# One more product in two levels, and three stages interleaved, in a linear-attention and tanh-shrink kernel

## Chip, cores, metric

The kernel runs on one core of one Trainium2 chip. The metric is the device time of one execution in microseconds; lower is better. Everything is f32.

## What is computed

The reference is a blockwise linear attention with decay, whose output, reordered to tokens by features, goes through a feed-forward block with the activation h - tanh(h):

```python
for b in range(nb):                                     # blocks of the sequence
    qb, kb, vb = (q[:, :, sl], k[:, :, sl], v[:, :, sl])
    intra = np.einsum('bhic,bhjc->bhij', qb, kb) * Dmask[None]
    intra = np.einsum('bhij,bhjd->bhid', intra, vb)
    inter = np.einsum('bhid,bhde->bhie', qb * lam_pow[None], kv_state)
    out[:, :, sl] = intra + inter
    kv_state = lam_block[None, :, None, None] * kv_state + np.einsum('bhsd,bhse->bhde', kb_dec, vb)
x = np.ascontiguousarray(attn_out.transpose(0, 2, 1, 3)).reshape(B * S, H * D)
h = x @ w_in
g = h - np.tanh(h)
return (g @ w_out).astype(np.float32)
```

Shapes: q, k and v are (4, 8, 768, 64), so x has 3072 tokens of 512 features; w_in is 512 x 2048 and w_out is 2048 x 512.

## The kernel before

The tokens are worked in six groups of 512 (128 positions of each of the 4 batches). While group g goes through the feed-forward block, attention for group g + 1 is run in pieces between its products: transposes and scores of two batches, then output and state, then the same for the other two (L381).

From group 1 on both matrix products use the Strassen-Winograd scheme: each operand is cut in 2 x 2 quarters, and seven products P1 to P7 of sums of quarters (`FACT`, L386) take the place of eight. Both the first product (tokens by w_in, `up`, L406) and the second (`down`, L602, and `down_twice`, L649) go that way. The first works per unit: there are NU = 4 units of 512 columns of w_in, and a product of one unit is 4 matmuls of 128 x 128 weights over 256 tokens. P1, P6 and P7 accumulate on one PSUM bank ("ya" or "yb"), P5 and P3 on "z"; what stands in a bank after each step is read by ScalarE or VectorE into the hidden tiles `hidden(g, c)`, with c = 11, 12, 21, 22 for the quarters of the result. The tanh and the subtraction are in `finish` (L421). Product P3 (L450) completes quarter 12, after which VectorE forms the sums S1 and S2 that the second product needs (L454, L455).

Some of the seven products are themselves computed by the same scheme a second time ("in two levels"): a product then consists of seven steps of 4 matmuls of 128 x 128 weights over 128 columns, in the order `STEPS = (1, 2, 6, 5, 7, 3, 4)`. In the second product these are P4 to P7 and P3 (`TWICE`), except some in the first and last groups; in the first product, from group GI = 2 on, they are P2 and P4 (`INNER`). `inner(g)` computes P2 and P4 together, a step of one and a step of the other in turn, before unit 0 starts. Weights for these steps that are sums of quarters are prepared once, in group 1, by `inner_weights` (L465) and written to DRAM (`fine_in`); the sums of tokens are formed per group by `inner_tokens` (L475).

Weights for the second product, and the sums for the steps 6, 5 and 3 of the two-level parts of the first, are streamed from DRAM as pieces of 256 KB in a ring of RING = 7 buffers. The order in which they are wanted is written out beforehand in `pieces_of` (L525); `piece` (L565) issues loads on POOL's queue up to seven pieces ahead. A buffer is loaded again when the matmuls that read it are done. Results are stored from POOL's queue too (L590). In the second product's P4 to P7 and P3, step x = 3 needs quarter a12 minus a sum, formed in place by VectorE at L666 after step 2 has read a12.

The order of the work in a group is the main loop's:

```python
for u in range(NU):
    for n in (2, 6, 5, 7, 1, 4, 3) if g < GI else (6, 5, 1, 7, 3) if u + 1 < NU else (6, 5, 7, 1, 3):
        ...            # n == 1: P1 of the next unit, and after the last unit the second product's P1
# then the second product: P2, P4, P5, P6, P7 with attention pieces between them, and
inner_tokens(g + 1)
down_twice(g, 3, "z")
inner(g + 1)
up(g + 1, 0, 1)
```

The instructions of each engine run in the order of its queue, which the tile framework makes from this program; operations marked `keep_in_program_order` stay where they are.

Of the kernel before, what the change touches and what calls it, by code (L numbers as in the profile page):

```python
# [23 lines left out]
def kernel(  # L24
# [32 lines left out]
    nc = tc.nc  # L57
# [129 lines left out]
    fine_in = dram.tile([2, 3, 128, NU, 128], F32, name="fine_in")  # L187
# [203 lines left out]
    def product_bank(key, n):  # L391

        if n == 1:
            banks[key, "y"] = bank("y", "yb" if key[0] == "up" and key[2] % 2 else "ya", 1)
        if n in (2, 5):
            banks[key, "zw"[n == 2]] = bank("zw"[n == 2], "zw"[n == 2], 1)
        t = banks[key, {2: "w", 5: "z", 3: "z"}.get(n, "y")]
        return t.rearrange("q (m c) -> q m c", m=2), n in (1, 2, 5)
# [7 lines left out]
    def up(g, u, n):  # L406
# [23 lines left out]
        elif g >= GI and n == 5:  # L430
            nc.scalar.activation(dst(22), z, AF.Copy)
        elif g >= GI and n == 7:
            nc.vector.tensor_tensor(dst(22), dst(22), y, op=AL.add)
            nc.vector.tensor_tensor(dst(21), dst(21), y, op=AL.add)
            finish(22, dst(22))
            finish(21, dst(21))
        elif n == 1:
            nc.scalar.activation(dst(11), y, AF.Copy)
        elif n == 2:
            nc.vector.tensor_tensor(dst(11), dst(11), w, op=AL.add)  # L440
            finish(11, dst(11))
        elif n == 6:
            nc.scalar.activation(dst(12), y, AF.Copy)
        elif n == 7:
            nc.scalar.activation(dst(22), y, AF.Copy)
            nc.vector.tensor_tensor(dst(22), dst(22), z, op=AL.add)
            finish(22, dst(22))
        elif n == 4:
            finish(21, y)
        elif n == 3:  # L450
            nc.vector.tensor_tensor(dst(12), dst(12), z, op=AL.add)
            finish(12, dst(12))

            nc.vector.tensor_tensor(dst("S1"), dst(12), dst(22), op=AL.add)  # L454
            nc.vector.tensor_tensor(dst(12), dst(11), dst(12), op=AL.subtract)  # L455
# [6 lines left out]
    def a_quarter(n, u, i, k):  # L462
        return w1[u][:, 2 + k, INNER.index(n), ts(i, 128)]

    def inner_weights(u):  # L465
        for n in INNER:
            a11, a12, a21, a22 = (a_quarter(n, u, i, k) for i in range(2) for k in range(2))
            t = late["pool"].tile([128, 4, 128], F32, name="ws2", tag="sums", bufs=4)
# [4 lines left out]
            nc.gpsimd.dma_start(out=fine_in[INNER.index(n)].rearrange("x p u c -> p u x c")[:, u], in_=t[:, 0:3])  # L473

    def inner_tokens(g):  # L475
        for n in INNER:
# [10 lines left out]
    def inner(g):  # L487

        y, w, z, r5 = {}, {}, {}, {}
        for n, tag in zip(INNER, ("yb", "ya")):  # L490
            y[n] = bank("y3", tag, 1)
            w[n], z[n] = (bank(x, "att", 4) for x in ("w3", "z3"))
            r5[n] = otile("r5")
        for x in STEPS:
            for n in INNER:
                out4 = hidden(g, 11 if n == 2 else 21)
                c11, c12, c21, c22 = (out4[:, :, i, ts(j, 128)] for i in range(2) for j in range(2))
                b = toks[g, n][x]
                wb = piece(g, ("in", n), x) if x in (3, 5, 6) else None
                dst = w[n] if x == 2 else z[n] if x in (3, 5) else y[n]  # L500
                for u in range(NU):
                    a = wb.rearrange("p m c -> p (m c)")[:, ts(u, 128)] if wb is not None else a_quarter(
                        n, u, *{1: (0, 0), 2: (0, 1), 7: (1, 0), 4: (1, 1)}[x])
                    nc.tensor.matmul(out=dst[:, ts(u, 128)], lhsT=a, rhs=b, start=x in (1, 2, 5) and u == 0, stop=True,  # L504
                                     skip_group_check=True)
                d = dst.rearrange("q (u c) -> q u c", u=NU)
                if x in (1, 4, 6):
                    nc.scalar.activation({1: c11, 4: c21, 6: c12}[x], d, AF.Copy)  # L508
                elif x == 5:
                    nc.scalar.activation(r5[n], dst, AF.Copy)  # L510
                elif x == 7:
                    nc.vector.tensor_tensor(c22, r5[n].rearrange("q (u c) -> q u c", u=NU), d, op=AL.add)
                else:
                    c = c11 if x == 2 else c12
                    nc.vector.tensor_tensor(c, c, d, op=AL.add)
# [8 lines left out]

    def pieces_of(g):  # L525
        if g >= GI:
            yield from ((g, ("in", n), x) for x in (6, 5, 3) for n in INNER)
        if g == 2:
            yield from ((g, ("quarter", t), x) for t in (3, 4) for x in range(4))
        for n in (1, 2, 4, 5, 6, 7, 3):  # L530
            yield from ((g, n, x) for x in (SUB if twice(g, n) else range(NU)))

# [32 lines left out]
    def piece(g, n, x):  # L565

        i = stream.index((g, n, x))
        while sent["n"] < min(i + RING, len(stream)):
# [5 lines left out]
            elif isinstance(n_, tuple):  # L574
                nc.gpsimd.dma_start(out=t.rearrange("p m c -> p (m c)"), in_=fine_in[
                    INNER.index(n_[1]), (5, 6, 3).index(x_)].rearrange("p u c -> p (u c)"))
# [24 lines left out]

    def down(g, n):  # L602

        if n in (1, 2):
            t, first = product_bank(("down", g), n)
        else:
            t, first = bank("plain", "w" if n == 7 else "z", 1).rearrange("q (m c) -> q m c", m=2), True
        a = hidden(g, HIDAT[FACT[n][0]])
        for u in range(NU):
            wb = piece(g, n, u)  # L610
            for m in range(2):
                for kt in range(2):
                    nc.tensor.matmul(out=t[:, m, :], lhsT=a[:, u, kt, ts(m, 128)], rhs=wb[:, kt, :],  # L613
                                     start=first and u == 0 and m == 0 and kt == 0, stop=u == NU - 1 and kt == 1,
                                     skip_group_check=True)
        t = t.rearrange("q m c -> q (m c)")
# [32 lines left out]
    def down_twice(g, n, zw):  # L649
# [6 lines left out]
        for x, a, dst, keep in ((1, a11, y, o[:, 0:128]), (2, a12, zw[:, 0:128], None), (6, s2, y, o[:, 128:256]),  # L656
# [8 lines left out]
            if x == 2:  # L665
                nc.vector.tensor_tensor(a12, a12, s2, op=AL.subtract)  # L666
        nc.vector.tensor_tensor(o[:, 384:512], o[:, 384:512], r5, op=AL.add)
# [11 lines left out]
        elif n == 3:  # L679
            nc.vector.tensor_tensor(o, o, res[g, 5], op=AL.add)  # L680
            store(g, 12, o)

# [83 lines left out]
    turns, made = {1: (0, (7, 14, 21)), 2: (7 * NU, (2, 7))}, []  # L766
# [3 lines left out]
    for g in range(1, NG):  # L770
        last = g == NG - 1
        p0, p1 = attention(g + 1) if not last else ([], [])
        for u in range(NU):
            for n in (2, 6, 5, 7, 1, 4, 3) if g < GI else (6, 5, 1, 7, 3) if u + 1 < NU else (6, 5, 7, 1, 3):
                if n != 1:
                    up(g, u, n)
                elif u + 1 < NU:
                    up(g, u + 1, 1)
                else:
                    down(g, 1)  # L780
# [10 lines left out]
            if g == GI - 1:  # L791
                inner_weights(u)
# [3 lines left out]
        down(g, 2)  # L796
        run(p0[2:])
        sums_twice(g, 5)
        down_twice(g, 4, "z")
# [3 lines left out]
        down_twice(g, 5, "w")  # L803
# [3 lines left out]
        down_twice(g, 6, "z")  # L807
# [3 lines left out]
        if twice(g, 7):  # L811
            down_twice(g, 7, "w")
        else:
            down(g, 7)
        if not last:
            if g + 1 >= GI:
                inner_tokens(g + 1)
            else:
                up(g + 1, 0, 1)
            if twice(g, 3):  # L820
                down_twice(g, 3, "z")
            else:
                down(g, 3)
            if g + 1 >= GI:
                inner(g + 1)
                up(g + 1, 0, 1)
        else:
            down_end(g)
# [30 lines left out]
```

## Time and profile before

| | us |
|---|---|
| median of 3 runs | 678.91 (676.9 to 679.36) |
| the profiled execution | 680.09 |
| its span | 678.3 |
| group 1 (155.2 to 265.4) | 110.2 |
| group 2 (265.4 to 371.5) | 106.1 |
| group 3 (371.5 to 477.8) | 106.3 |
| group 4 (477.8 to 582.0) | 104.2 |
| group 5 (582.0 to 678.0) | 96.0 |

Each group is counted from its first matmul of the first product (for group 1, of the first unit). The granted TensorE clock was 1.00 in all five. DMA moved 129.59 MB; 256 KB pieces took a median of 4.1 us (two-level weights of the second product), 4.4 (one-level) and 5.4 (fine_in) from issue to landing.

How to read the lines quoted later. A group line names source line, engine, operation, what is written and read, the shape and the count. A line of the timeline has start and length in us, then the engine, line and operation; in brackets stands the idle time of the engine before it and what ended it. A line of the windows has the stretch and its length, then the busy time of TensorE, of its weight loads (PEld), VectorE (DVE), ScalarE (ACT) and GpSimd (POOL), the granted clock, the busy share of the DMA engines and GB/s.

### The profile page before, as it was taken

To read this page: it belongs to the slowest core of one execution; us is meant where nothing else is said; L and a number is where in the kernel's file an instruction comes from. 1 tells how busy PE (TensorE), PEld (TensorE's weight loads), DVE (VectorE), ACT (ScalarE), POOL (GpSimd) and SP (SyncE) were. 2 spreads that over 40 slices of the span, in tenths; PEclk is the share of its full clock that TensorE was granted. 3 is DMA by queue.
4 is the path that set the end of the run, shared out by engine and by line. 5 is a ranking of instruction groups with operands and counts; after the bars stand their busy time and mean duration, and the time that the engine had idled before them with its cause. 6 is when DMAs were issued, how large, how long until landed. Compare 5 with 4: busy or idle time off the path is not lost.

```text
span 678.3 us, 12940 instructions
## 1 busy us (share of the span) xinstructions
PE 662.7 (98%) x4832; PEld 575.2 (85%) x4832; DVE 482.0 (71%) x878; ACT 201.3 (30%) x398; POOL 201.5 (30%) x348
## 2 busy tenths in 40 slices
PE   6899999999999999999999999999999999999997
PEld 5788855558888899988999988899988899988897
DVE  3797858894889962588986378887358977357753
ACT  2664432423331211343112343112333122334120
POOL 0001424216444434421345200255300244500261
PEclk9999999999999999999999999999999999999999
DMA  9869979958957978686698641698821676700494
GB/s 187 227 195 236 287 215 257 301 142 248 263 173 215 259 208 202 160 238 136 180 277 266 192 82 43 153 284 244 246 42 36 153 240 206 249 22 1 112 303 159
DMA packets 162957, 129.59 MB, mean 191 GB/s; under 512 B 133904, under 2 KB 135056, under 8 KB 162896
## 3 DMA queue, kind: packets, MB, share of 16 engines
q0 software_dynamic: 29216, 97.28, 45.6%
q1 hardware_dynamic: 133536, 31.50, 23.4%
q8 instruction: 38, 0.62, 0.4%
q14 instruction: 23, 0.19, 0.1%
q10 hardware_dynamic: 144, 0.00, 0.0%
HBM read 104.34 MB, written 24.38 MB: 190 GB/s over the span
## 4 chain that ended last, share of the span: by engine, by line
PE 69%; issue 15%; POOL 6%; DMA 6%; DVE 3%; ACT 1%; SPq 0%; POOLq 0%; DVEq 0%; ACTq 0%
PE y L415 13%; PE op L719 8%; PE z L415 8%; PE y L661 7%; PE h L703 6%; PE zw L661 5%; POOL wb L578 5%; PE y L504 3%; PE w L613 3%; PE y L613 3%; PE sp L313 3%; DMA wb<-fine 2%; PE plain L613 2%; DMA raw<-in_moe_w_in_dram 2%; PE op L364 2%
## 5 line engine op out<-in xcount | busy, mean ns | idle before, releaser
L578 POOL DMA_DIRECT2D wb<-fine x154 | 82.9, 538 | 122.0 <-PE y L661 46.3
L423 ACT ACTIVATE th<-g 128x512 f32<-128x512 f32 x76 | 47.3, 630 | 104.5 <-DVE g L428 35.6
L581 POOL DMA_DIRECT2D wb<-factors x52 | 28.2, 543 | 162.0 <-PE y L613 118.1
L415 PE MATMUL y<-xt,w 128*128 128x256 f32 x320 | 73.5, 380 | 0.0
L415 PEld LDWEIGHTS y<-xt,w 128*128 128x128 f32 x320 | 60.5, 190 | 9.4 <-ACT g L508 0.9
L424 DVE TENSOR_TENSOR g<-g,th 128x512 f32<-128x512 f32 x76 | 52.0, 689 | 22.5 <-ACT th L423 22.2
L664 ACT ACTIVATE q<-y 128x128 f32<-128x128 f32 x88 | 24.4, 277 | 115.8 <-PE y L661 114.0
L703 PE MATMUL h<-xt,w 128*128 128x256 f32 x256 | 56.2, 381 | 1.1 <-DVE w L270 1.1
L719 PE MATMUL op<-wt,g 128*128 128x512 f32 x128 | 56.5, 596 | 0.0
L703 PEld LDWEIGHTS h<-xt,w 128*128 128x128 f32 x256 | 48.3, 190 | 8.5 <-DVE w L270 1.5
L661 PE MATMUL y<-wb,g 128*128 128x128 f32 x408 | 54.4, 278 | 1.0 <-DMA wb<-fine 1.0
L661 PEld LDWEIGHTS y<-wb,g 128*128 128x128 f32 x408 | 49.3, 192 | 2.4 <-issue 1.5
L719 PEld LDWEIGHTS op<-wt,g 128*128 128x128 f32 x128 | 23.8, 190 | 27.7 <-issue 26.5
L415 PE MATMUL z<-tt,ws 128*128 128x256 f32 x160 | 38.7, 380 | 0.0
L317 DVE TENSOR_TENSOR ss<-sp,mask 128x512 f32<-128x512 f32 x48 | 30.8, 681 | 10.6 <-PE sp L313 10.6
L415 PE MATMUL y<-tt,ws 128*128 128x256 f32 x160 | 38.2, 382 | 0.0
L415 PE MATMUL z<-xt,ws 128*128 128x256 f32 x160 | 37.9, 380 | 0.0
L661 PE MATMUL zw<-wb,g 128*128 128x128 f32 x272 | 36.1, 276 | 0.6 <-DMA wb<-fine 0.5
L197 POOL DMA_DIRECT2D raw<-in_moe_w_out_dram x16 | 8.8, 553 | 92.7 <-ACT r L261 59.9
L613 PE MATMUL w<-wb,g 128*128 128x256 f32 x160 | 35.8, 382 | 0.0
L613 PE MATMUL y<-wb,g 128*128 128x256 f32 x160 | 35.4, 379 | 0.0
L415 PEld LDWEIGHTS y<-tt,ws 128*128 128x128 f32 x160 | 30.1, 190 | 5.4 <-DVE g L428 1.5
(169 smaller groups left out, 1290.5 us busy)
## 6 DMA issues: line engine op xcount, KB each, us to landing
wb<-fine POOLq DMA_DIRECT2D x154, 256.0 KB, 4.1
wb<-factors POOLq DMA_DIRECT2D x60, 256.0 KB, 4.4
raw<-in_moe_w_out_dram POOLq DMA_DIRECT2D x16, 512.0 KB, 5.1
v_nat<-in_v_dram SPq DMA_DIRECT2D x24, 256.0 KB, 5.3
factors<-wt POOLq DMA_DIRECT2D x8, 768.0 KB, 5.5
wb<-fine_in POOLq DMA_DIRECT2D x24, 256.0 KB, 5.4
k_nat<-in_k_dram SPq DMA_DIRECT2D x20, 256.0 KB, 5.4
raw<-in_moe_w_in_dram SPq DMA_DIRECT2D x8, 512.0 KB, 5.8
```

Source lines behind the costliest of these rows:

```text
L313: nc.tensor.matmul(out=sp[j][:, p, :], lhsT=kt[ts(j, 64), p, :], rhs=qt[ts(j, 64), p, :], start=True, stop=True)
L317: nc.vector.tensor_tensor(ss[:, j], sp[j], mask[:, j], op=AL.mult)
L415: nc.tensor.matmul(out=t[:, m, :], lhsT=wt[:, kt, ts(m, 128)], rhs=x[:, kt, :], start=first and m == 0 and kt == 0, stop=kt == 1, skip_gro ...
L423: nc.scalar.activation(th, src, AF.Tanh)
L424: nc.vector.tensor_tensor(dst(c), src, th, op=AL.subtract)
L578: nc.gpsimd.dma_start(out=t.rearrange("p m c -> p (m c)"), in_=fine[TWICE.index(n_), SUB.index(x_)].rearrange("p u c -> p (u c)"))
L581: nc.gpsimd.dma_start(out=t, in_=factors[XAT[FACT[n_][1]]][:, 2 * x_:2 * x_ + 2, :])
L613: nc.tensor.matmul(out=t[:, m, :], lhsT=a[:, u, kt, ts(m, 128)], rhs=wb[:, kt, :], start=first and u == 0 and m == 0 and kt == 0, stop=u = ...
L661: nc.tensor.matmul(out=dst, lhsT=a[:, u, :], rhs=wb[:, ts(u, 128)], start=x in (1, 2) and u == 0, stop=u == NU - 1, skip_group_check=True)
L664: nc.scalar.activation(keep, dst, AF.Copy)
L703: nc.tensor.matmul(out=hm[:, m, :], lhsT=w1[u][:, i, a, ts(m, 128)], rhs=xt[0, t][:, i, :], start=m == 0 and i == 0, stop=i == KI - 1, ski ...
L719: nc.tensor.matmul(out=obank[b], lhsT=g, rhs=wt[:, 2 * a:2 * a + 2, :], start=kt == 0 and a == 0, stop=kt == KH - 1 and a == 1)
```

## The change

P3 of the first product is computed in two levels from group 2 on. It leaves the unit loop; its seven steps are run once for all four units, in turn with the four units of the second product's P1 (`inner_last`). P2 of the next group is run in turn with P3 of the second product, step by step (`in_turn`), and P4 of the next group in turn with P1, P6 and P5 of its unit 0 and P1 of its unit 1. The weight stream is reordered to match. The sums of weights for P3 are written by `inner_weights` in group 1, its sums of tokens are formed at unit 1. The addition of P5 to quarter 12, part of P3's work before, moves to P5 in the unit loop. The banks of the unit's products change ("w", "ya", "yb", "w" for units 0 to 3), and the last two sets of second-product weights made in group 2 get their turns at other places. `down` and `down_twice` become generators, so that a caller can take one step at a time.

```diff
     def product_bank(key, n):
         if n == 1:
-            banks[key, "y"] = bank("y", "yb" if key[0] == "up" and key[2] % 2 else "ya", 1)
+            tag = "ya" if key[0] == "down" else ("w", "ya", "yb", "w")[key[2]] if key[1] >= GI else ("ya", "yb")[key[2] % 2]
+            banks[key, "y"] = bank("y", tag, 1)
...
         elif g >= GI and n == 5:
             nc.scalar.activation(dst(22), z, AF.Copy)
+            nc.vector.tensor_tensor(dst(12), dst(12), z, op=AL.add)
...
-    def inner(g):
+    def inner_step(g, n, x, dst):
+        b = toks[g, n][x]
+        wb = piece(g, ("in", n), x) if x in (3, 5, 6) else None
+        for u in range(NU):
+            a = wb.rearrange("p m c -> p (m c)")[:, ts(u, 128)] if wb is not None else a_quarter(
+                n, u, *{1: (0, 0), 2: (0, 1), 7: (1, 0), 4: (1, 1)}[x])
+            nc.tensor.matmul(out=dst[:, ts(u, 128)], lhsT=a, rhs=b, start=x in (1, 2, 5) and u == 0, stop=True,
+                             skip_group_check=True)
+        return dst.rearrange("q (u c) -> q u c", u=NU)
+
+    def inner_steps(g, n, tag):
+        y, w, z, r5 = bank("y3", tag, 1), bank("w3", "att", 4), bank("z3", "att", 4), otile("r5")
...
+    def inner_last(g):
+        y, w, z = (bank("y3", "yb", 1), bank("w3", "w", 1), bank("z3", "z", 1))
+        def quarter_of(c, i, j):
+            return hidden(g, c)[:, :, i, ts(j, 128)]
+        for step in (0, (1, 0, 0), (2, 0, 0), 1, (6, 0, 1), (5, 1, 1), 2, (7, 1, 1), (3, 0, 1), 3, (4, 1, 0)):
+            if isinstance(step, int):
+                down_unit(g, 1, step)
+                continue
+            x, i, j = step
+            c = quarter_of(12, i, j)
+            d = inner_step(g, 3, x, w if x == 2 else z if x in (3, 5) else y)
+            nc.vector.tensor_tensor(c, c, d, op=AL.add)
+            if x in (2, 7, 3, 4):
+                th = work.tile([128, NU, 128], F32, name="th2", tag="th")
+                nc.scalar.activation(th, c, AF.Tanh)
+                nc.vector.tensor_tensor(c, c, th, op=AL.subtract)
+                nc.vector.tensor_tensor(quarter_of("S1", i, j), c, quarter_of(22, i, j), op=AL.add)
+                nc.vector.tensor_tensor(c, quarter_of(11, i, j), c, op=AL.subtract)
+        down_end_of(g, 1)
...
+    def in_turn(g):
+        if twice(g, 3):
+            return [a for x in STEPS for a in (("down", x), ("in", x))]
+        return [("down", 0), ("in", 1), ("in", 2), ("down", 1), ("in", 6), ("in", 5), ("down", 2), ("in", 7), ("in", 3),
+                ("down", 3), ("in", 4)]
...
     def pieces_of(g):
         if g >= GI:
-            yield from ((g, ("in", n), x) for x in (6, 5, 3) for n in INNER)
+            yield from ((g, ("in", 4), x) for x in (6, 5, 3))
...
-        for n in (1, 2, 4, 5, 6, 7, 3):
+        for n in (1, 2, 4, 5, 6, 7):
+            if g >= GI and n == 1:
+                yield from ((g, 1, 0), (g, 1, 1), (g, ("in", 3), 6), (g, ("in", 3), 5), (g, 1, 2), (g, ("in", 3), 3),
+                            (g, 1, 3))
+                continue
             yield from ((g, n, x) for x in (SUB if twice(g, n) else range(NU)))
...
+        for kind, x in in_turn(g):
+            if kind == "down":
+                yield g, 3, x
+            elif x in (3, 5, 6):
+                yield g + 1, ("in", 2), x
...
-    turns, made = {1: (0, (7, 14, 21)), 2: (7 * NU, (2, 7))}, []
+    turns, made = {1: (0, (7, 14, 21)), 2: (7 * NU, (1, 5))}, []
...
-            for n in (2, 6, 5, 7, 1, 4, 3) if g < GI else (6, 5, 1, 7, 3) if u + 1 < NU else (6, 5, 7, 1, 3):
+            if g >= GI and u == 1:
+                inner_tokens(g, (3,))
+            for n in (2, 6, 5, 7, 1, 4, 3) if g < GI else (7,) if u == 0 else (6, 1, 5, 7) if u + 1 < NU else (
+                    6, 5, 7, 1):
                 if n != 1:
                     up(g, u, n)
+                elif g >= GI and u + 1 == NU:
+                    inner_last(g)
...
             if g == GI - 1:
-                inner_weights(u)
+                inner_weights(u, INNER)
+                for uu in ((), (), (0, 1), (2,))[u]:
+                    inner_weights(uu, (3,), False)
...
-            if twice(g, 3):
-                down_twice(g, 3, "z")
-            else:
-                down(g, 3)
-            if g + 1 >= GI:
-                inner(g + 1)
-                up(g + 1, 0, 1)
+        inner_tokens(g + 1, INNER)
+        p3 = down_twice(g, 3, "z") if twice(g, 3) else down(g, 3)
+        p2 = inner_steps(g + 1, 2, "yb")
+        for kind, _ in in_turn(g):
+            next(p3 if kind == "down" else p2)
+        every(p2)
+        every(p3)
+        p4 = inner_steps(g + 1, 4, "yb")
+        for n in (None, None, 1, None, None, 6, None, None, -1, None, 5):
+            if n is None:
+                next(p4)
+            else:
+                up(g + 1, n < 0, abs(n))
+        every(p4)
```

`inner_steps` reads the banks as `inner` did; the sums of weights of the last unit for P3 are made after the second product's P4 in group 1. New code places L666 of `down_twice` at L722.

## The prediction

> **What bounds the kernel now.** I read the busy table first, then the windows of one group, then TensorE's timeline inside it, and VectorE's and the DMAs' only where TensorE loses time.
>
> ```profile
> PE 662.7 (98%) x4832; PEld 575.2 (85%) x4832; DVE 482.0 (71%) x878; ACT 201.3 (30%) x398; POOL 201.5 (30%) x348
> ```
> ```profile
> 265.40:371.50 106.10, 105.93 (x874) 97.36 (x873) 81.57 (x139) 28.44 (x61) 39.51 (x69) 1.00 0.76 207
> ```
>
> The second line is group 2, from its first two-level matmul to that of group 3: TensorE 105.93 of 106.10 us, VectorE 81.57. But VectorE's mean hides a stretch from 306 to 334 us in which it pauses for well under 2 us. Two prices come from TensorE's timeline:
>
> ```profile
> 311.30 7.07 PE L613 MATMUL y<-wb,g 128*128 128x256 f32 x32
> 318.21 1.89 PE L415 MATMUL z<-xt,ws 128*128 128x256 f32 x8
> 371.45 1.06 PE L504 MATMUL y<-xt,w 128*128 128x128 f32 x8
> 372.34 1.06 PE L504 MATMUL y<-tt,w 128*128 128x128 f32 x8
> ```
>
> An f32 matmul leaves two records. From start to start, 32 records of 256 columns take 318.21 - 311.30 = 6.91 us, so a unit's product (4 matmuls) costs 1.73; 8 records of 128 columns take 0.89, the price of a two-level step (4 matmuls). Time above these prices is what TensorE lost. Three places matter:
>
> ```profile
> 277.86 1.03 PE L415 MATMUL z<-tt,ws 128*128 128x256 f32 x4
> 278.72 1.98 PE L415 MATMUL y<-xt,w 128*128 128x256 f32 x8
> 280.54 1.03 PE L415 MATMUL z<-tt,ws 128*128 128x256 f32 x4
> 281.54 1.99 PE L415 MATMUL y<-tt,ws 128*128 128x256 f32 x8
> 283.37 3.62 PE L415 MATMUL y<-xt,w 128*128 128x256 f32 x16
> ...
> 476.80 1.13 PE L661 MATMUL y<-wb,g 128*128 128x128 f32 x8 [0.98 <-DMA wb<-fine]
> ```
> ```profile
> 234.75 0.71 DVE L293 STREAM_TRANSPOSE kt<-k_blk 128x512 f32<-128x512 f32 x1 [1.41 <-DMA k_nat<-in_k_dram]
> 235.39 0.65 DVE L303 TENSOR_TENSOR qd<-qt,fwd 128x512 f32<-128x512 f32 x1
> 235.96 0.68 DVE L666 TENSOR_TENSOR gS<-gS,s 128x512 f32<-128x512 f32 x1
> ...
> 335.07 0.69 DVE L666 TENSOR_TENSOR g<-g,s 128x512 f32<-128x512 f32 x1 [0.59 <-PE zw L661]
> ```
>
> Unit 0: P5, P1, P6 need 24 records x 0.216 = 5.18 us and take 283.37 - 277.86 = 5.51. Weights: the last step of the second product's P3 in group 3 waits for its load. VectorE: in group 1 TensorE's next step x=3 starts at 236.74, just after the L666 at 235.96 that it needs, so there VectorE already sets the pace. In group 2 the same instruction waits for TensorE.
>
> **What the Trainium skill says.** "Perfetto Trace Analysis", Identifying the Most-Contended Engine, holds matmul busy time a poor measure and points to LDWEIGHTS; here that row is 85%, and the even start-to-start times show TensorE full all the same. "TensorE: Matmul & The Clock Gate", Back-to-back issue gap, has the spacing of short matmuls set by the weight load as well, so that half the columns cost more than half; the trace agrees in kind (0.216 against 0.111 a record). "VectorE: DVE Perf Modes", The perf-mode tier table, keeps f32 tensor_tensor at its base rate from SBUF and PSUM alike; the trace agrees (689 ns on L424 from SBUF, 0.69 on L451 from PSUM, some 0.60 between starts in a full queue). "DMA: Bandwidth & Descriptors", Anatomy of one DMA, gives 2.0 us plus bytes over 436 GB/s, an estimate of 2.6 us for 256 KB; the trace has 4.1 for the two-level weights and decides.
>
> **The change part by part.**
>
> 1. *P3 in two levels, groups 2 to 5.* Removed: 4 units x 1.73 = 6.91 us a group. Added: 7 steps x 0.89 = 6.25. TensorE is the path, so 4 x -0.66 = **-2.6 us**.
>
> 2. *P4 in turn with unit 0, and no P3 in the unit loop.* P6 of unit 0 then has two P4 steps (1.79 us) between itself and P1, whose L428 must first read the bank; the 0.33 us above goes, and it is the same in groups 3, 4 and 5: 1.3, I take -1.2. P5 also waits for its bank z before unit 2 in groups 2 and 4 (0.30 and 0.23 over price), because P3 sat in that bank; now P5's result leaves by one copy and one addition, three products ahead: -0.5. Together **-1.7** (0 to -1.8).
>
> 3. *P3 of the second product in turn with P2.* Now 7 weight pieces in 6.25 us, then 6 in the 12.5 us of P2 and P4 together. After: 10 pieces in the first 12.5 us, 3 in P4. A ring of 7 gives a load 7 steps, 6.25 us; waiting on POOL and issue take about 0.9 of them, and landing 4.1 (5.9 in the bad case). Spread out it has about 8.7. So the 1.15 us of group 3 and 0.37 of group 2 mostly go: **-1.2** (0 to -1.6). The stores of q4 and q7 stay where they were in POOL's queue behind the weights; P2's r5 copy needs q4's slot, whose store is issued at 366.70 and lands 4.8 later, about 371.5; that copy comes 7.1 us after P7's end at 364.8, so 371.9, and TensorE needs it only 2.7 us after that. Free, with cover.
>
> 4. *VectorE's queue in groups 2 to 4.* Per group 16 operations leave the units (four of L451 to L455 in each); in come 4 additions of z in the units, 7 of steps, and 3 for each of 4 quarters: 23. Worse than 7 x 0.60 is where they go: 19 of them stand in P3's 13.2 us with P1 (7 x 0.89 + 4 x 1.73), besides unit 3's leftovers. Walking the compiled order of group 3 from the end of unit 3's P7 (time 0) at 0.60 an operation: the transposes begin at -2.4 instead of -0.8; P7's two reads end at 3.05, and step x=2, which reuses their bank, can start at 3.5: 0.4 to spare. The scores' products end at 19.8 (wanted at 23.4), both k_nat at 24.0 (wanted 25.3), L666 of P4 at 30.7 (wanted 30.9), and that of P5, behind six operations of the transposes, at 37.8 (wanted 37.2). So 0.6 us of stall in groups 2 and 3; in group 4 there is no state to update (four operations, 2.4 us, fewer; there L666 waits 2.26 us for TensorE now), so none. **+1.2** (0 if operations overlap better; +4 if the queue is a microsecond later).
>
> 5. *Group 1: three times the inner weights.* 16 more small operations (281 ns long, 0.20 between starts), 12 of them before the scores, 2.4 us in a VectorE queue that hardly pauses from 195 to 230; 1.3 us of pauses near 210 absorb about half. The two L666 at 227.60 and 235.96 both already hold TensorE, so what remains lands on it. The 4 extra writes of fine_in (0.75 us each on POOL) stand ahead of weight pieces, each waiting for its VectorE operations. **+1.5** (0 to +3). The 12 more loads and 4 writes, about 3.9 MB of 129.6, fall mostly where the DMA row reads 42 to 82 GB/s: nothing. The later turn of the last two factors costs nothing, their VectorE work only changes unit.
>
> 6. *New waits.* Steps of P3 alternate with P1's units, so a bank gets 2.6 us between two writes, against 0.7 for a read. ScalarE is 30% busy. In P4 the bank of P2 is taken over after one step (0.89) against a copy of 0.60 plus its start. I take **+0.5** for a few tenths lost somewhere (0 to +2).
>
> Sum: -2.6 - 1.7 - 1.2 + 1.2 + 1.5 + 0.5 = -2.3. The profiled execution took 680.09 us (span 678.3 and 1.8 around it), so 677.8; the median shown is 678.91, 1.2 less, which puts the forecast at **676.6**.
>
> **The rivals.**
>
> *All of it hides.* VectorE's pauses take up parts 4 to 6. For: VectorE at 71% over the span. Against: the stretch from 306 to 334 us. 678.91 - 5.5 + 0.2 = 673.6.
>
> *The waits of unit 0 and of the weights only move.* Then parts 2 and 3 bring nothing: -2.6 + 3.2 = +0.6, 679.5. For: the DMA row is at 244 to 284 GB/s in the stages of the two-level second product, which stay. Against: the steps that waited are now apart.
>
> *VectorE becomes the bound after P3 (slower).* The place is L666 of P4 and P5 in groups 2, 3 and 4. My walk leaves it no reserve, so every further microsecond of lag is one of TensorE's. An operation that depends on the one before it starts 0.72 us after it (L454 to L455: 300.54 to 301.27), not 0.60, and a quarter's chain crosses ScalarE, 1.44 us from addition to subtraction. If half the 19 pay for it, about 2.5 us a group: three groups +7.5, and 678.91 - 2.3 + 7.5 = 684.1. It decides from 1.9 us a group on (3.4 + 2.3 over 3). Against: the compiled order mixes quarters so that few neighbours depend on each other.
>
> That the change doesn't do what it says is excluded: TensorE's compiled order has the 28 short matmuls for the 16.
>
> **How the numbers follow.** 0.5% is 3.4 us, about what a measurement of this kernel can tell from no change. Forecast 0.42 (own range 675 to 679), all hidden 0.22, waits move 0.14, VectorE binds 0.22. A sixth of the forecast's chance lies beyond -3.4 (0.07) and a little of two cases beyond +3.4 (0.03): faster 0.29, same 0.46, slower 0.25. Range 673 to 683: below it is a part of the second case, above it the worse half of the last.
>
> **What would show it.** Right: the P3 steps at 0.89 start to start; P5, P1, P6 of unit 0 without loss; no DMA named before the last step of the second product's P3; group 1 longer by 1 to 2 us. Wrong: pauses of TensorE over 1 us named to L722 (the new line of L666) or to a bank read in P3, or weights of fine_in landing late.

## The result, and the profile after

The changed kernel took 679.82 us (median of 22 runs, 678.29 to 684.59) against 678.60 for the kernel before, measured beside it (22 runs): a ratio of 1.0028, 95% interval 1.0015 to 1.0041. Forecast were 2.3 us less; it is 1.2 to 1.9 us more, depending on whether medians or the ratio are taken. Run again, beside other kernels, it gave 1.0026 (1.0012 to 1.0040).

Time is easiest to compare between two marks that both kernels have: the start of P7 of the second product of each group. "Group 1" below runs from its first unit product to P7; "rest" from the last P7 to the last matmul. What lies ahead of group 1 is left out: it took 153.6 to 156.4 us in the profiles of this study and differs from profile to profile, though almost nothing there was changed. The kernel before has one profile, after has two. The numbers are differences of start times in TensorE's timelines, in us.

| kernel | group 1 | 1 to 2 | 2 to 3 | 3 to 4 | 4 to 5 | rest | sum |
|---|---|---|---|---|---|---|---|
| before | 96.3 | 107.0 | 105.5 | 104.5 | 92.6 | 13.8 | 519.7 |
| after | 99.0 | 107.7 | 104.8 | 103.1 | 91.6 | 14.9 | 521.1 |
| after, run again | 97.5 | 107.7 | 105.2 | 103.1 | 92.0 | 14.6 | 520.2 |

So the ways from 2 to 3, from 3 to 4 and from 4 to 5 did become shorter, by 0.7, 1.4 and 0.9 us (in the second profile of after by 0.3, 1.4 and 0.6); group 1, the way from 1 to 2 and the rest give it back. TensorE's loss, the sum of what its starts exceed the two prices of the prediction, says the same: it rose from 14.5 to 18.5 us, so the 2.66 us of saved matmul time are outweighed.

The page's busy line of after, then the windows of the first two stretches:

```profile
PE 660.6 (97%) x4928; PEld 578.1 (85%) x4928; DVE 503.6 (74%) x938; ACT 200.0 (29%) x398; POOL 211.4 (31%) x364
```
```profile
155.14:254.10 98.96, 94.94 (x713) 84.65 (x711) 75.47 (x159) 24.08 (x49) 48.77 (x79) 1.00 0.84 240
254.10:361.90 107.80, 106.22 (x853) 97.53 (x849) 82.70 (x142) 25.70 (x52) 38.02 (x66) 1.00 0.75 204
```

TensorE's share fell by one point while VectorE got 60 more operations. In group 1 TensorE is idle 4.0 of 98.96 us, in the next stretch 1.6.

**Unit 0**, TensorE's timeline of after:

```profile
276.16 1.89 PE L416 MATMUL y<-xt,w 128*128 128x256 f32 x8
277.89 1.05 PE L496 MATMUL y<-tt,wb 128*128 128x128 f32 x8
278.78 1.06 PE L496 MATMUL z<-tt,wb 128*128 128x128 f32 x8
279.67 1.89 PE L416 MATMUL y<-tt,ws 128*128 128x256 f32 x8
```

From start to start 1.73, 0.89 and 0.89: no loss between P1 and P6, in any group. **The bank z** in group 2 is another matter. TensorE first, then VectorE:

```profile
303.07 1.89 PE L416 MATMUL y<-tt,ws 128*128 128x256 f32 x8
305.42 1.78 PE L416 MATMUL z<-tt,ws 128*128 128x256 f32 x7 [0.45 <-DVE g L433]
```
```profile
301.77 0.69 DVE L606 TENSOR_TENSOR wt<-wb,wt 128x512 f32<-128x512 f32 x1 [0.18 <-DMA fine<-wt]
302.38 0.68 DVE L606 TENSOR_TENSOR wb<-wb 128x512 f32<-128x512 f32 x1
303.47 0.69 DVE L606 TENSOR_TENSOR wt<-wb,wt 128x512 f32<-128x512 f32 x1 [0.41 <-DVE wb L606]
304.08 0.69 DVE L425 TENSOR_TENSOR g<-g,th 128x512 f32<-128x512 f32 x1
304.68 0.68 DVE L433 TENSOR_TENSOR g<-g,z 128x512 f32<-128x512 f32 x1
```

L606 forms the last set of two-level weights. Its first line here waits 0.18 us for a store that must free a buffer. The line at 303.47 stands idle for 0.41 us; the profile puts this down to the L606 before it, but in the four such lines from 292.12 us on there is no such gap, so a second store is the likelier cause. Everything behind in VectorE's queue waits too: L433, the addition that reads bank z, ends only at 305.36, and P5 of unit 2 follows at once.

**VectorE and L722.** TensorE in P4 and P5 of the second product in group 2, then VectorE:

```profile
338.93 1.06 PE L717 MATMUL y<-wb,g 128*128 128x128 f32 x8
340.70 1.13 PE L717 MATMUL zw<-wb,g 128*128 128x128 f32 x8 [0.72 <-ACT q L720]
...
347.61 1.13 PE L717 MATMUL zw<-wb,gS 128*128 128x128 f32 x8 [0.41 <-ACT q L720]
```
```profile
339.92 0.68 DVE L722 TENSOR_TENSOR g<-g,s 128x512 f32<-128x512 f32 x1
...
346.83 0.68 DVE L722 TENSOR_TENSOR gS<-gS,s 128x512 f32<-128x512 f32 x1
```

The wait is put down to ScalarE's L720, but that copy was done long before; what ends last is L722, which TensorE's step needs (339.92 + 0.68 = 340.60, and the step starts at 340.70). Before, VectorE waited 0.59 us for TensorE at the first of these places; now TensorE waits.

**Group 1**, the same two steps and the state's matmuls, then VectorE:

```profile
224.54 0.69 PE L333 MATMUL kv<-v_nat,k_nat 128*64 128x64 f32 x16 [0.47 <-DVE k_nat L328]
...
230.60 1.13 PE L717 MATMUL zw<-wb,g 128*128 128x128 f32 x8 [0.72 <-ACT q L720]
...
239.67 1.13 PE L717 MATMUL zw<-wb,gS 128*128 128x128 f32 x8 [2.16 <-DVE gS L722]
```
```profile
237.68 0.71 DVE L293 STREAM_TRANSPOSE kt<-k_blk 128x512 f32<-128x512 f32 x1 [1.08 <-DMA k_blk<-in_k_dram]
238.31 0.65 DVE L303 TENSOR_TENSOR qd<-qt,fwd 128x512 f32<-128x512 f32 x1
238.88 0.68 DVE L722 TENSOR_TENSOR gS<-gS,s 128x512 f32<-128x512 f32 x1
```

The first two waits are VectorE's, behind the small operations of the sums of weights. The third stands behind a transpose that waits for a block of k to land; the kernel before has such a wait in the same place (1.41 us).

**The rest.** GpSimd's queue, then TensorE:

```profile
656.47 0.54 POOL L623 DMA_DIRECT2D wb<-fine  x1 [0.36 <-PE y L717]
659.80 3.18 POOL L623 DMA_DIRECT2D wb<-fine  x6 [2.79 <-PE y L717]
```
```profile
662.89 1.13 PE L717 MATMUL zw<-wb,g 128*128 128x128 f32 x8 [0.47 <-DMA wb<-fine]
...
665.71 1.16 PE L717 MATMUL zw<-wb,s 128*128 128x128 f32 x8 [0.80 <-DMA wb<-fine]
```

Until 656.47 GpSimd issues a load every 0.89 us, as TensorE frees a slot. Then it stands still for 2.79 us although slots come free, and issues six loads back to back. Two of them come too late. Counted from the start of the trace, the pause follows GpSimd's 348th DMA. Nothing in the prediction foresaw it.

### The profile page after: what moved, and what is told of

Same layout as the page of the kernel before. It is cut to its first block, busy times and chain, and to the rows that moved or that the text cites. A ratio compares the mean times of both kernels' runs of the same rounds, so it can differ in the third digit from the quotient of the medians.

```text
span 679.7 us, 13243 instructions
## 1 busy us (share of the span) xinstructions
PE 660.6 (97%) x4928; PEld 578.1 (85%) x4928; DVE 503.6 (74%) x938; ACT 200.0 (29%) x398; POOL 211.4 (31%) x364
## 4 chain that ended last, share of the span: by engine, by line
PE 66%; DMA 11%; issue 10%; SPq 6%; POOL 3%; DVE 2%; ACT 1%; POOLq 0%; DVEq 0%; ACTq 0%
PE y L717 9%; PE h L766 8%; PE y L416 7%; PE zw L717 7%; SPq L141 6%; DMA k_blk<-in_k_dram 5%; PE y L496 5%; PE op L782 5%; PE w L658 3%; PE y L658 3%; PE z L496 3%; PE sp L313 3%; PE z L416 3%; PE op L364 2%; PE plain L658 2%
## 5 line engine op out<-in xcount | busy, mean ns | idle before, releaser
L416 PE MATMUL y<-xt,w 128*128 128x256 f32 x320 | 75.1, 379 | 0.0
L424 ACT ACTIVATE th<-g 128x512 f32<-128x512 f32 x60 | 37.2, 630 | 92.4 <-DVE g L435 35.8
L720 ACT ACTIVATE q<-y 128x128 f32<-128x128 f32 x88 | 24.4, 278 | 124.3 <-PE y L717 123.4
L425 DVE TENSOR_TENSOR g<-g,th 128x512 f32<-128x512 f32 x60 | 40.1, 689 | 17.6 <-ACT th L424 17.4
L197 POOL DMA_DIRECT2D raw<-in_moe_w_out_dram x16 | 8.9, 555 | 92.6 <-DVE g L770 54.3
L658 PE MATMUL y<-wb,g 128*128 128x256 f32 x160 | 37.7, 379 | 0.0
L717 PEld LDWEIGHTS zw<-wb,g 128*128 128x128 f32 x272 | 33.1, 192 | 2.5 <-ACT q L720 1.8
L416 PEld LDWEIGHTS z<-tt,ws 128*128 128x128 f32 x160 | 30.0, 190 | 4.7 <-DVE g L433 0.9
```

What stands on the lines that cost most here:

```text
L416: nc.tensor.matmul(out=t[:, m, :], lhsT=wt[:, kt, ts(m, 128)], rhs=x[:, kt, :], start=first and m == 0 and kt == 0, stop=kt == 1, skip_gro ...
L424: nc.scalar.activation(th, src, AF.Tanh)
L425: nc.vector.tensor_tensor(dst(c), src, th, op=AL.subtract)
L717: nc.tensor.matmul(out=dst, lhsT=a[:, u, :], rhs=wb[:, ts(u, 128)], start=x in (1, 2) and u == 0, stop=u == NU - 1, skip_group_check=True)
```

## The experiments

Every kernel was timed beside the kernel before on its own chip; ratios are against that. Two theories stood at first, that VectorE's queue holds TensorE after P3 and in group 1, and that the loss is in DMAs which come late; from the second run of after on, that GpSimd's pause carries part of it.

| run | median us | before | ratio, 95% interval |
|---|---|---|---|
| sums of weights late | 678.39 | 678.32 | 1.0001 (0.9988 to 1.0015) |
| four operations of VectorE fewer | 678.78 | 678.32 | 1.0007 (0.9989 to 1.0025) |
| P2 and P4 not in turn | 680.53 | 678.32 | 1.0034 (1.0018 to 1.0050) |
| P3 in one level | 676.93 | 678.32 | 0.9973 (0.9961 to 0.9985) |
| after, run again | 680.19 | 678.58 | 1.0026 (1.0012 to 1.0040) |
| quarter loads by SyncE | 694.24 | 678.58 | 1.0235 (1.0199 to 1.0272) |
| attention early | 682.24 | 678.58 | 1.0050 (1.0033 to 1.0068) |
| later turn | 683.23 | 678.58 | 1.0075 (1.0046 to 1.0105) |
| from group 3, ScalarE writes | 692.51 | 678.44 | 1.0210 (1.0181 to 1.0239) |
| output stores by ScalarE | 691.91 | 678.44 | 1.0206 (1.0183 to 1.0230) |
| P3 in one level, P2 after P3 | 677.66 | 678.44 | 0.9991 (0.9979 to 1.0003) |
| from group 3, GpSimd writes | 675.36 | 678.96 | 0.9949 (0.9933 to 0.9964) |

**Sums of weights late.** The sums for P3 are made at the end of group 1 instead of within it.

```diff
-                for uu in ((), (), (0, 1), (2,))[u]:
-                    inner_weights(uu, (3,), False)
...
         inner_tokens(g + 1, INNER)
+        if g == GI - 1:
+            for u in range(NU):
+                inner_weights(u, (3,), False)
```

> The changed kernel, with the 16 small VectorE operations and the 4 writes that make P3's inner weights moved from the middle of group 1 to its end, after the tokens' sums for group 2, where VectorE pauses; their buffers are those of the transposes. Theory V (VectorE's full queue in group 1 hands its delay to TensorE): group 1 up to the start of the second product's P3 falls by about 2.7 us, to the 103.2 of the kernel before, and the time to about 677.1. Rival D (the extra DMA traffic and the new order of the weights cost the time): the writes and loads are all still there, so 679.8 stays.

It ran level with the kernel before. In its profile the first two waits of group 1 are gone (0.26 us is left of the second, as before) and group 1 takes 97.2 us, though one weight is 0.8 late in it; the third wait is still there (1.8), again behind a block of k, and the way to group 2 is as long as after's (107.7). So the small operations do hold TensorE, for about 1.7 us (1.1 at the state's matmuls, 0.6 at L722); the third wait of group 1 comes without them too.

**Four operations of VectorE fewer.** One of the three operations that follow the addition in each quarter of P3 is left out, the subtraction of tanh, so this part of the activation is missing.

```diff
             if x in (2, 7, 3, 4):
                 th = work.tile([128, NU, 128], F32, name="th2", tag="th")
                 nc.scalar.activation(th, c, AF.Tanh)
-                nc.vector.tensor_tensor(c, c, th, op=AL.subtract)
```

> The changed kernel without the subtraction of the tanh in quarter 12 in the new P3 (4 of VectorE's 19 operations there, groups 2 to 5; that part of the activation is left out). Theory V: 2.4 us less in the queue end the waits of TensorE for L722's subtraction, 0.88 and 0.58 us in group 2 and 0.5 in group 3, so about 677.9. Rival D: the waits are for weights, 679.8 stays.

With four operations fewer, 2.4 us of VectorE's time, both waits for L722 in group 2 are gone: from the scores to P7 it takes 38.3 us instead of 39.6. This shows that it is the length of VectorE's queue that holds them. In group 3 it is otherwise: L722 now ends 1.2 us before the step that needs it (449.37 against 450.53), yet that step still starts 0.6 us late, for a reason that the profile doesn't show. The gain is also smaller than expected, because the wait for bank z grew to 1.9 us, which keeps the way from group 1 to 2 at 107.7 us, and the pause near the end is there. That wait fits its cause: the two idle gaps of VectorE at the sums of weights are 0.97 and 0.92 us here, together as long as TensorE's wait.

**P2 and P4 not in turn.** P2 and P4 run in turn with each other after P3 of the second product, as before the change; P3 of the first product stays in two levels.

```diff
-        for kind, _ in in_turn(g):
-            next(p3 if kind == "down" else p2)
-        every(p2)
         every(p3)
-        p4 = inner_steps(g + 1, 4, "yb")
-        for n in (None, None, 1, None, None, 6, None, None, -1, None, 5):
...
+        p4 = inner_steps(g + 1, 4, "ya")
+        for _ in STEPS:
+            next(p2)
+            next(p4)
+        every(p2)
+        every(p4)
+        for n in (1, 6, -1, 5):
+            up(g + 1, n < 0, abs(n))
```

> The changed kernel with P2 and P4 in turn with each other again, after the second product's P3 and before unit 0; P3 in two levels stays. If the two interleavings bring what the two traces show (0.33 us at unit 0 in four groups, about 1.0 us of late weights), the time rises by about 2.3, to 682.1. Rival (the waits only move): 679.8 stays, with as much lost elsewhere.

680.5, nearer to the rival. Its ratio of 1.0034 can't be told from after's (1.0028 and 1.0026). By stretch the four ways from P7 to P7 add up to 408.7 us, against 407.2 and 408.0 in the two profiles of after. By these single profiles the turns brought some 1 us in this kernel (0.7 to 1.5), not 2.3 and more.

**P3 in one level.** Both turns stay; P3 of the first product goes back into the units, and with it the sums of weights and of tokens, the addition L433 and twelve weight loads.

```diff
-            for n in (2, 6, 5, 7, 1, 4, 3) if g < GI else (7,) if u == 0 else (6, 1, 5, 7) if u + 1 < NU else (
-                    6, 5, 7, 1):
+            for n in (2, 6, 5, 7, 1, 4, 3) if g < GI else (7, 3) if u == 0 else (6, 5, 1, 7, 3) if u + 1 < NU else (
+                    6, 5, 7, 1, 3):
...
-                elif g >= GI and u + 1 == NU:
-                    inner_last(g)
```

> The changed kernel with P3 in one level per unit again, as before, without its inner weights and tokens; both interleavings stay. Theory V: loses the 2.6 us of TensorE that two levels save, and wins back 2.7 in group 1, about 1.9 after P3 and 0.6 at unit 3's P5: about 677.2, so that P3 in two levels is a net loss of about 2.6. Rival 1 (VectorE has no part in it): 679.8 + 2.6 = 682.4. Rival 2 (28 short matmuls are not cheaper than 16 on TensorE): below 675.

As expected from the theory of VectorE: 676.9, 0.27% below the kernel before. The turns, with the changed banks and the moved turn of the last weights, bring 1.8 us (1.0 to 2.6) of the 2.9 that parts 2 and 3 of the prediction said, and it is P3 in two levels that loses: 2.66 us of matmuls saved, and the time still 3.7 us longer (1.0028 less 0.9973 is 0.55%).

**After, run again**, with three changes to it, each aimed at one of the four places.

> The changed kernel unaltered, beside the three that follow. If its loss is in fixed places, the same ones show up: VectorE's queue in group 1 (from the first unit of group 1 to P7 of its second product 97.5 to 99.0 us against 96.3 before), waits of TensorE for VectorE's L722 in group 2 (0.88 and 0.58 us) and 3 (0.51), the wait for bank z ahead of P5 of unit 2 in group 2 (0.6 or more), and GpSimd's pause of 2.8 us after its 348th DMA near 657 us, with late weights behind it. About 679.8 us. If these are chance, at most two of them come back.

All came back: group 1 97.5 us; L722 0.88 and 0.58 in group 2, 0.50 in group 3; bank z 0.62; the pause after the 348th DMA, up to 659.2 us, with two late weights behind it. They are places, not chance, except for part of group 1, which was 1.5 us shorter.

**Quarter loads by SyncE.**

```diff
-                nc.gpsimd.dma_start(out=x, in_=quarter_source(t, i, j))
+                nc.sync.dma_start(out=x, in_=quarter_source(t, i, j))
```

> The twelve quarter loads of group 1 (L598) are issued by SyncE instead of GpSimd, which is left with 346 DMAs. Theory (the pause near 657 us belongs to the count of DMAs that GpSimd has issued): no pause of 2.8 us there, weights in time, 13.3 us instead of 14.9 from the start of the last P7 to the end, 1.2 us off the time, about 678.6. Rival (256 KB every 0.89 us is more than the DMAs carry): weights late there as before, 679.8.

On the pause the theory is right: none near the end, no late weights, and the rest takes 13.4 us (expected 13.3). It now follows the 278th DMA, at 572 us, where it costs nothing that can be seen. The 278th is 30 later than the 248th, after only twelve DMAs fewer, so it isn't DMAs alone that are counted: these twelve are of short pieces (512 bytes), and each weighs as much as several loads. An earlier pause stands behind the 179th, at 381 us. The last section comes back to this. The kernel as a whole is 2.4% slower for another reason: SyncE's queue holds the attention blocks, and their first load slipped from 148.6 to 185.3 us; group 1 and the way to group 2 together are 17 us longer than in the second run of after.

**Attention early.**

```diff
-            if not last and u > 1:
-                run(p0[u - 2:u - 1])
+            if not last and u > (1 if g < GI else 0):
+                run(p0[u - (2 if g < GI else 1):][:1] if u < 3 or g < GI else [])
```

> In groups 2 to 4 the transposes and the scores of the next group stand one unit earlier (units 1 and 2 instead of 2 and 3), so five of VectorE's operations and more leave the stretch in which P3 is computed. Theory (VectorE's queue is late only there): the waits for L722 in groups 2 and 3 (0.88, 0.58 and 0.51 us) go, 1.8 us off, about 678.0. Rival (VectorE has no room in the units either): the waits appear in the units, 679.8 or more.

The rival. The waits for L722 shrank to 0.3 us, but the scores stood 2.4 us waiting in the units of group 2:

```profile
307.04 3.87 PE L313 MATMUL sp<-qt,kt 64*128 64x128 f32 x32 [2.44 <-DVE kt L293]
```

The transposes were queued behind L606 there, which waits for its stores. This place in group 2 had no room in VectorE's queue; no other was tried.

**Later turn.**

```diff
-    turns, made = {1: (0, (7, 14, 21)), 2: (7 * NU, (1, 5))}, []
+    turns, made = {1: (0, (7, 14, 21)), 2: (7 * NU, (1, 9))}, []
```

> The last set of two-level weights made in group 2 gets its turn four products later (after P7 of unit 2). Theory (VectorE stands at its subtractions, L606, waiting for the stores that free their buffers, and the addition L433 behind them holds bank z): P5 of unit 2 in group 2 no longer waits, 0.6 us off, about 679.2. Rival (bank z is held by the addition itself, or the wait for stores only moves): the wait is there still or comes in P3, 679.8 or more.

The wait for bank z is gone, which confirms its cause, but the second product's P1 now waits for its weights: the four quarters that L606 reads hold their slots of the ring longer (GpSimd's load at 307.62 us had waited 4.93 us for L606). TensorE loses 1.3 us at L722 of P5 instead of 0.58:

```profile
314.35 0.70 PE L658 MATMUL y<-wb,g 128*128 128x256 f32 x2 [1.33 <-DMA wb<-factors]
```

**From group 3, ScalarE writes; output stores by ScalarE.** In the first of these two, P3 is in two levels in groups 3 to 5 only, and its sums are made near the end of group 2; both give the four output stores of group 0 to ScalarE, the first also the writes of the sums.

```diff
-            nc.gpsimd.dma_start(out=fine_in[n - 2].rearrange("x p u c -> p u x c")[:, u], in_=t[:, 0:3])
+            (nc.gpsimd if small else nc.scalar).dma_start(out=fine_in[n - 2].rearrange("x p u c -> p u x c")[:, u], in_=t[:, 0:3])
...
-                nc.gpsimd.dma_start(out=out[b * S:b * S + BLK, :], in_=ob)
+                nc.scalar.dma_start(out=out[b * S:b * S + BLK, :], in_=ob)
```

> P3 of the first product in two levels from group 3 on only; in group 2 it stays in the units, in one level. Its sums of weights are made and written (by ScalarE) near the end of group 2, where VectorE pauses (368 to 372 us); the four first output stores go to ScalarE as well, so that GpSimd's pause falls where it has nothing to load. Theory (the loss is VectorE in groups 1 and 2 and GpSimd's pause, not P3 in two levels): from the kernel with P3 in one level everywhere, at 676.9, three groups at 0.66 come off and 0.3 for the sums comes on: 675.2. Rival (P3 in two levels is paid back by VectorE wherever it stands): 676.9 or more, with waits for L722 over 0.5 us in groups 3 and 4 beyond those of the kernel with P3 in one level.

> The changed kernel with the four first output stores (128x512, near 157 us) issued by ScalarE instead of GpSimd. Theory (GpSimd's pause comes after a fixed amount of what it has issued): both pauses come four loads later, again behind its 248th and 348th DMA by the new count; the last one at about 660.6 us instead of 657, with six loads left instead of ten, and the time from the start of the last P7 to the end falls from 14.6 to about 14.0. About 679.4 us against 680.0. Rival (the pauses belong to what TensorE or the DMAs do then): they stay at 471 and 657 us, and the time stays.

They missed by 17.3 and 12.5 us, and for a reason that neither theory had. With the stores on ScalarE, SyncE's first attention block went out at 160.2 us instead of 148.6. SyncE then issues blocks without a pause, so the delay arrives whole in group 1, where a transpose waits 8.13 us for a DMA and TensorE 9.2 us behind it. The writes of the sums by ScalarE stood in the way in group 2:

```profile
386.44 0.43 ACTq L478 DMA_DIRECT2D fine_in<-ws  x1
386.92 0.60 ACT L511 ACTIVATE g<-y 128x512 f32<-128x512 f32 x1 [8.71 <-DMA q_blk<-in_q_dram]
```

ScalarE waited for a block that SyncE was loading, with the copies of P2 behind it; TensorE lost 6.1 us. As to the pause, the second kernel has it after the 347th DMA by the new count, where 348 was expected, so it did come three loads later and belongs to what GpSimd has issued; the rest got no shorter (14.8). From P7 of group 3 to P7 of group 5 the first kernel takes 102.1 and 92.2 us, 1.3 us less than the kernel with P3 in one level (195.6), which is what two products in two levels should bring (2 x 0.66); the rest takes 13.1.

**P3 in one level, P2 after P3.**

```diff
-        if twice(g, 3):
-            return [a for x in STEPS for a in (("down", x), ("in", x))]
-        return [("down", 0), ("in", 1), ("in", 2), ("down", 1), ("in", 6), ("in", 5), ("down", 2), ("in", 7), ("in", 3),
-                ("down", 3), ("in", 4)]
+        return [("down", x) for x in (STEPS if twice(g, 3) else range(NU))] + [("in", x) for x in STEPS]
```

> The kernel with P3 in one level, but with P2 of the next group behind P3 of the second product instead of in turn with it; P4 stays in turn with unit 0. If the turns relieve the weights of P3, these come late again: TensorE waits for DMAs in P3 of groups 2 and 3, about 1.2 us more, 678.1. If the turns of P2 and P3 bring nothing and unit 0 is all the gain: 676.9.

In between (677.7), but not as either side had it. No step of P3 loses over 0.25 us, although P3 stands alone again; what is lost are 0.4 us a group in P2, whose steps now write bank y one right after another; that this is the cause is likely, but was not tried by itself.

**From group 3, GpSimd writes.** The kernel that should follow if the reading above is right.

```diff
+    def inner_weights_3(u):
+        if u == 0:
+            for x, tag in enumerate(("qt", "kt", "qd")):
+                sums3[x] = work.tile([128, NU, 128], F32, name="ws3", tag=tag)
...
+        if u == NU - 1:
+            for x in range(3):
+                nc.gpsimd.dma_start(out=fine_in[1, x], in_=sums3[x])
...
-        eng = nc.sync if g == NG - 1 else nc.gpsimd
+        eng = nc.sync if g == NG - 1 or g == NG - 2 and c != 11 else nc.gpsimd
```

> P3 of the first product in two levels from group 3 on, as in the run before, but with nothing added to SyncE's or ScalarE's queues while attention blocks are loaded: the first output stores stay with GpSimd, the sums of weights for P3 are gathered for all units and written by GpSimd in three DMAs near the end of group 2, and three stores of group 4, when SyncE has no more blocks to load, go to SyncE. Theory (what the change loses is VectorE in groups 1 and 2 and GpSimd's pause near the end): 2.0 us under the kernel with P3 in one level (676.9), 0.3 for the sums, 675.2; group 1 within 0.5 us of before, no wait over 0.3 us before P7 of the second product in group 5 nor after it. Rival (P3 in two levels is paid back wherever it stands): 676.9 or more.

675.4 us, 0.51% (0.36 to 0.67) below the kernel before, against the 675.2 expected, and the fastest of all. The kernel with P3 in one level, which the rival wanted it not to beat, had 0.9973 (0.9961 to 0.9985); the intervals just touch, so the times alone speak narrowly against the rival, and the stretches agree with them. Its stretches are 95.9, 106.6, 104.8, 102.1, 92.3 and 13.1 us, in sum 514.8. Against the kernel with P3 in one level the way from 2 to 3 is 0.7 us shorter and the two behind it together 1.2, 1.9 us of the 2.0 that three products should bring. L722 still costs 0.5 us in group 3. One wait is longer than expected, 0.6 us at the start of P5 in group 5, put down to a weight. The pause is still there, after the 253rd DMA, and no load behind it is late:

```profile
476.74 0.54 POOL L636 DMA_DIRECT2D wb<-fine_in  x1 [0.36 <-PE zw L733]
480.07 0.54 POOL L636 DMA_DIRECT2D wb<-fine_in  x1 [2.80 <-PE zw L733]
```

## Why the prediction was wrong

Most of the mechanisms were named, but parts 2, 3 and 4 were mis-sized, part 5 was exceeded in one profile, and one term was put at nothing. TensorE's losses in the profile of after, less those of before, give each term its size; where the second profile of after differs, its value stands in brackets. The losses of before are those of a single profile.

- *Part 1, -2.6:* right, 2.66 us of matmuls gone.
- *Part 2, -1.7:* the 0.33 us of unit 0 went in all four groups (-1.3), but bank z was released later in group 2, 0.72 lost instead of 0.31, and in group 4 about 0.2 stays, now in a step of P3. It came to -0.9. The step that failed is "now P5's result leaves by one copy and one addition, three products ahead": the addition stands in VectorE's queue behind L606, and L606 behind its stores. Of the moved turn the prediction said that it "costs nothing, their VectorE work only changes unit". The later turn, with that wait gone, showed the cause.
- *Part 3, -1.2:* -0.9. In group 3 0.7 us of late weights remain, behind GpSimd's pause near 473 us: the steps at 483.05 and 484.27 wait for loads issued right after it. That the turns cured the lateness of before isn't shown: with P3 in one level and no turns (P2 after P3) it didn't come back, and with P3 in two levels and no turns one step of P3 lost 0.9 us, behind the pause.
- *Part 4, +1.2:* +1.8 (2.3). The walk through group 3 was good for its first L722 (0.2 us lost) and its second (0.6, as worked out). What failed is "So 0.6 us of stall in groups 2 and 3": in group 2, 1.5 us were lost at the two L722, where VectorE comes out of the units later than in group 3. The walk was made in one group and carried to another whose queue holds L606.
- *Part 5, +1.5:* +2.6 (1.1), about 1.7 of it tied to the small operations by the run with late sums. The size was right: over the profiles of this study group 1 takes 98.0 us on average with the small operations in it (six profiles) and 96.1 without (four). The remainder is the third wait, which differs from profile to profile (0.8 to 2.2 in those of this study). For its place the prediction had misread a line: the L666 at 235.96 us stands behind 1.41 us idle for a block of k, so VectorE's queue didn't set the pace there, and part of the added work fitted into that gap.
- *Part 6, +0.5:* about 0.2, in pieces of 0.06.
- *Missing, +1.1 (0.8):* GpSimd's pause. Part 5 put the 16 added DMAs at "nothing", by the DMA engines' load. Their cost is in the issuing queue: with them the first pause comes earlier (471.7 us instead of 483.6, ahead of group 3's P3 instead of behind it), and a second falls into the last P7, where every load has only 6.25 us. Before, GpSimd issues too little ever to reach the second. In the eight profiles with a pause behind the last P7's loads the rest takes 14.1 to 15.1 us, in the six others 13.1 to 13.8.

Together -2.66 - 0.9 - 0.9 + 1.8 + 2.6 + 0.2 + 1.1 = +1.2; the table has +1.4. Of the rivals, "VectorE becomes the bound after P3" had the right place, but in group 2 alone and below its threshold of 1.9 us a group; "the waits of unit 0 and of weights only move" was right for bank z and half right for the weights. The doubt that the prediction stated for the stretch from 306 to 334 us was the right one.

What stays open: what the pause of GpSimd is; what starts the step behind L722 in group 3 late when four operations are gone; and whether late weights as in before's group 3 are common or were one profile's.

## What to carry to other kernels

A saving of TensorE's that is paid in operations of a nearly full queue has to be walked through in every stage where it lands: the same edit cost 0.5 us at one step of group 3, next to nothing in groups 4 and 5, and more than it saved in groups 1 and 2, and applying it only where the queue had room gave the best kernel. Before moving an instruction, look at what it waits for, and at who stands behind it: a subtraction that waits for a store held a bank three instructions further back. Added DMAs are to be counted on the queue that issues them as well as in bytes.

## What the runs showed of the hardware

GpSimd stands still for about 2.8 us at points that depend on what it has issued so far: after its 248th and 348th DMA in after, run twice, and in five variants of it that issue as many DMAs up to there, its 252nd in before, its 278th where twelve loads of short pieces were taken from it, its 253rd in the last kernel.

These counts fall together when one counts rows, that is contiguous pieces of a DMA's destination (128 of 2 KB in a weight of 256 KB, 512 of 512 bytes in a quarter load). Up to the 248th, 252nd, 253rd and 278th DMA of these kernels GpSimd has issued 54,656 to 54,912 rows. The 348th ends 13,696 rows after the 248th, and the earlier pause of the kernel with loads by SyncE comes 13,696 rows before its 278th DMA. Before issues 66,816 rows in all, after 69,888, so before doesn't reach a second pause. At the first two multiples of about 13,700 rows no clear pause is seen, nor where GpSimd waits for something else anyway. The Trainium skill, "DMA: Bandwidth & Descriptors", SWDGE vs HWDGE vs iDMA, has GpSimd write descriptors into rings in SBUF; a ring that comes round would fit, but no run here shows that it is the cause.

DMAs issued by ScalarE and by SyncE were not independent: ScalarE's write waited 8.7 us, until a block of SyncE's had landed, and four stores on ScalarE delayed SyncE's blocks by 11.6 us. The traces put this down to semaphores of the program. The stores on ScalarE landed at 153.58, 155.52 and 160.09 us, and SyncE's next loads, which waited for the semaphores of these stores, went out at 153.66, 155.54 and 160.17; ScalarE's write at 386.44 went out after a load of SyncE's had landed at 386.36.
